# RetNet recurrence and SwiGLU block on one core: first chunk's scores first, and a new table of times for the later stages

## The chip, the cores and the metric

The kernel runs on one core of one Trainium2 chip. The metric is the device time of one execution, in microseconds (us). The engines are named as in the profile: PE is TensorE's matrix multiply and PEld its load of weights, DVE is VectorE, ACT is ScalarE, POOL is GpSimd, SP is SyncE, whose queue issues all the DMA transfers of this kernel. Each engine works through its own list of instructions in order; an instruction that waits holds up all behind it on the same engine.

## The reference

Two blocks follow one another. The first is a RetNet recurrence over 4 batches, 8 heads, 768 positions and 64 features of a head; the second is a SwiGLU feed-forward block on the 3072 x 512 matrix that comes out of it.

```python
gamma = 1.0 - 2.0 ** (-5.0 - np.arange(H))
scale = 1.0 / np.sqrt(D)
for t in range(S):
    state = gamma[None, :, None, None] * state + np.einsum('bhd,bhe->bhde', k[:, :, t], v[:, :, t])
    y[:, :, t] = scale * np.einsum('bhd,bhde->bhe', q[:, :, t], state)
# (B,H,S,D) -> (B*S, H*D), then
g = x @ w_gate                       # 3072 x 1536
silu = g * (1.0 / (1.0 + np.exp(-g)))
out = (silu * (x @ w_val)) @ w_out   # 3072 x 512
```

q, k and v are float32, the three weight matrices float64.

## The kernel before

**Chunks and segments.** The recurrence is done in chunks of 128 positions (6 to a batch): *scores* of a chunk (keys against queries, times a decay mask), a *mix* (scores against values, plus the decayed query against the state before), and a new *state* (decayed keys against values). A segment is 3 chunks of each of 2 batches; there are 4 segments, s = 0 to 3. Each goes through an *up* stage (gate and value products, 12 groups f of 128 hidden columns) and a *down* stage (12 groups f against six tiles of 128 tokens, `tok`). The attention of segment s + 1 is laid between the matmuls of the down stage of segment s. So the time runs: opening (attention of segment 0), up 0, down 0, up 1, down 1, up 2, down 2, up 3, down 3.

**Opening and first up stage.** The order of the opening is the string `START`. Each word is a step of `parts`: `l2:1` loads operand 1 of chunk number 2 (0 is k transposed, 1 q transposed, 2 v, 3 k), `A0` a slice of the table of decays (`tabs`), `s` scores, `m` mix, `t` state, `K`/`k` and `Q`/`q` the scaling of keys and queries by decays (capital: on DVE, small: on POOL), `g` the decay of a state, `x0:1` one sum of x, `U1:2` the load of weight piece 1 into buffer place 2, `a`, `b`, `S`, `c`, `C` the steps that turn float64 words into float32 (`a`, `b`, `c` on ACT, `S` on DVE, `C` on POOL), `T` sums of weights, `w6` six matmuls of filler. The table of decays is `tab`: columns 0 to 1023 are the mask, in two halves of 512 for the two heads of a pair, then the decays of queries and keys. `scores` (L412) does 16 matmuls into two banks and then two DVE multiplies (L424), one for each half of the mask; there are two banks for scores of all chunks. The first up stage (`up`, L653, matmuls L663) multiplies in plain float32; between its products `beside` names what else is done, mostly the conversion of the weights. A load that overwrites a buffer waits in SP's queue until the last reader is through, and all loads behind it wait as well.

**Later stages.** Matmuls run in a faster 32-bit form on operands cut in three parts. Weights and hidden values are cut by `near_a` (ACT, L718), `near_b` (DVE, L721) and `near_c` (POOL, L724, or DVE, L80); x is cut by `far_a` to `far_d` (ACT L727, DVE L80, DVE L733, ACT L739). An up stage (`up3`, L828, matmuls L824) does seven products for each f in the order 1, 2, 6, 5, 7, 3, 4, of 6 matmuls each, after a scheme that saves one product in eight; the results are added up by `p1`, `u2`, `p5` (ACT copies, L839 to L841), `c11`, `h1`, `h0` (DVE additions), and two silus and two multiplies:

```python
        steps = (lambda: copy(p1, x), lambda: tt(c11, z, p1, op=add),
                 lambda: act(gate, c11, AF.Silu, scale=ONE), lambda: copy(u2, x),
                 lambda: copy(p5, wb), lambda: tt(h1, x, p5, op=add),
                 lambda: tt(h0, wb, u2, op=add), lambda: tt(h0, h0, gate, op=mul),
                 lambda: act(x, x, AF.Silu, scale=ONE), lambda: tt(h1, h1, x, op=mul))
        for d, step in zip(WHEN["u", 3 if f == NF - 1 else min(f, 2)], steps):
            at(t + d, step)
```

Products 6, 7 and 4 add to the bank of product 1, so product 6 waits for p1's copy and product 7 for u2's. Split weights and hidden values take turns in four buffers (`item("g", ...)`).

**What sets the order.** `at(t, fn)` files a step under a time; `run()` emits all steps sorted by it. These times are not waits: they only say in which order each engine has its instructions. The table `WHEN` has the times, as offsets from the start of the work they belong to: `('u', i)` the ten steps above (i is f, 2 for f from 2 to 10, 3 for the last), `('w', i, g)` the three steps of cutting weight group g, `('h', f)` those of hidden group f before `down`, `('s', p, g)`, `('m', p)`, `('y', p)`, `('old', p)`, `('new', p)`, `('sum', p)` and `('far', p, n)` what follows scores, mix and state of the p-th pair of chunks in a down stage, `'end'` and `'last'` the evictions of the down stage's results. Before the change nearly all keys of one kind have the same times.

Of the kernel before, what the change touches and what calls it, by code (L numbers as in the profile page):

```python
# [49 lines left out]
def tile_retnet_swiglu(  # L50
# [233 lines left out]
    def do(order):  # L284
# [7 lines left out]
        l0:0 l0:1 A0 l1:0 l1:1 l0:2 l1:2 A1 l0:3 l2:0 l2:1 l1:3 l2:2 l2:3 l3:0 l3:1 l3:2  # L292
        l3:3 l4:0 l4:1 U0:0 l4:2 l5:0 l5:1 l5:2 l4:3 l5:3 s1 s0 K0 m1 w6 k2 K1 t0 m0 s2 t1
        g3 Q2 g2 x0:0 x0:1 s3 U1:2 q3 m2 m3 t2 x1:0 k3 a0 x0:2 x0:3 t3 b0 x1:1 s4 S0 q4 x1:2
        c0 s5 q5 x1:3 m4 C0 m5 a1 x2:0 U3:4 T0:0 x2:1 T0:1 U2:0 T0:2 x2:2 x2:3 U12:6
# [30 lines left out]
        ('u', 0): (1.15, 2.19, 2.89, 3.24, 4.29, 5.33, 6.38, 7.08, 7.43, 8.13),  # L326
        ('u', 1): (1.15, 2.19, 2.89, 3.24, 4.29, 5.33, 6.38, 7.08, 7.43, 8.13),
        ('u', 2): (1.15, 2.19, 2.89, 3.24, 4.29, 5.33, 6.38, 7.08, 7.43, 8.13),
        ('u', 3): (1.15, 2.19, 2.89, 3.24, 4.29, 5.33, 6.38, 7.08, 7.43, 8.13),
        ('w', 0, 0): (-9.0, -7.4, -6.2),  # L330
        ('w', 0, 1): (-9.0, -7.4, -6.2),
        ('w', 0, 2): (-9.0, -7.4, -6.2),
        ('w', 1, 0): (-7.2, -5.6, -4.4),
        ('w', 1, 1): (-7.2, -5.6, -4.4),
        ('w', 1, 2): (-7.2, -5.6, -4.4),
        ('w', 2, 0): (-7.2, -5.6, -4.4),
        ('w', 2, 1): (-7.2, -5.6, -4.4),
        ('w', 2, 2): (-7.2, -5.6, -4.4),
        ('h', 0): (-7.5, -6.3, -5.3),
        ('h', 1): (-7.5, -6.3, -5.3),  # L340
        ('h', 2): (-7.5, -6.3, -5.3),
        ('h', 3): (-7.5, -6.3, -5.3),
        ('h', 4): (-7.5, -6.3, -5.3),
        ('h', 5): (-7.5, -6.3, -5.3),
        ('h', 6): (-7.5, -6.3, -5.3),
        ('h', 7): (-7.5, -6.3, -5.3),
        ('h', 8): (-7.5, -6.3, -5.3),
        ('h', 9): (-7.5, -6.3, -5.3),
        ('h', 10): (-7.5, -6.3, -5.3),
        ('h', 11): (-7.5, -6.3, -5.3),  # L350
        ('s', 0, 0): (0.0, 0.0),
        ('s', 0, 1): (0.0, 0.0, 0.0, 0.0),
        ('m', 0): (0.0, 0.0, 0.0),
        ('y', 0): (0.0, 0.0, 0.0, 0.0, 0.0, 0.0, 0.0, 0.0),
        ('old', 0): 2.4,
        ('new', 0): 0.0,
        ('sum', 0): (2.6, 3.0, 3.4, 3.8),
        ('far', 0, 1): (2.8, 4.6, 5.2, 6.0),
        ('far', 0, 2): (3.5, 5.8, 6.2, 6.8),
        ('far', 0, 0): (4.2, 6.5, 9.2, 10.6),  # L360
        ('s', 1, 0): (0.0, 0.0),
        ('s', 1, 1): (0.0, 0.0, 0.0, 0.0),
        ('m', 1): (0.0, 0.0, 0.0),
        ('y', 1): (0.0, 0.0, 0.0, 0.0, 0.0, 0.0, 0.0, 0.0),
        ('old', 1): 2.4,
        ('new', 1): 0.0,
        ('sum', 1): (2.6, 3.0, 3.4, 3.8),
        ('far', 1, 1): (2.8, 4.6, 5.2, 6.0),
        ('far', 1, 2): (3.5, 5.8, 6.2, 6.8),
        ('far', 1, 0): (4.2, 6.5, 9.2, 10.6),  # L370
        ('s', 2, 0): (0.0, 0.0),
        ('s', 2, 1): (0.0, 0.0, 0.0, 0.0),
        ('m', 2): (0.0, 0.0, 0.0),
        ('y', 2): (0.0, 0.0, 0.0, 0.0, 0.0, 0.0, 0.0, 0.0),
        ('old', 2): 2.4,
        ('new', 2): 0.0,
        ('sum', 2): (2.6, 3.0, 3.4, 3.8),
        ('far', 2, 1): (2.8, 4.3, 4.9, 5.6),
        ('far', 2, 2): (3.5, 5.2, 5.6, 6.0),
        ('far', 2, 0): (4.2, 6.1, 6.9, 8.0),  # L380
        'end': (0.1, 0.1, 0.1, 0.1, 5.0, 5.0),
        'last': (0.1, 0.1, 0.1, 0.1, 0.1, 0.1),
# [671 lines left out]
```

## Time and profile before

| | before |
|---|---|
| time, median of 3 | 695.98 us (695.15 to 696.91) |
| span of the profiled execution | 691.8 us, 12321 instructions |
| PE busy | 666.2 us (96%), 4724 matmuls |
| PEld busy | 551.0 us (80%) |
| DVE busy | 474.9 us (69%), 742 instructions |
| ACT busy | 382.5 us (55%), 793 instructions |
| POOL busy | 250.3 us (36%), 164 instructions |
| DMA | 141.58 MB, 205 GB/s over the span |
| granted PE clock | 1.00 throughout |

The span is the time from the first to the last instruction that the profiler saw. Busy times of different engines overlap. A busy PE isn't PE at its peak, since matmuls are pipelined and their ends are modelled; a wait between two groups of matmuls shows as idle time or as a longer group. The stages can be told by PE's lines: L418 to L478 opening, L663 first up stage, L874 with L520 a down stage with attention, L824 a later up stage.

### The profile page before, as it was taken

The numbers are of one execution on the slowest core, as the hardware profiler recorded it, in microseconds if no ns is written. First come the engines' busy times: TensorE is split into PE (matmuls) and PEld (weight loads), VectorE is DVE, ScalarE is ACT, GpSimd is POOL, SyncE is SP. The second block draws the span as 40 slices with busy tenths as digits, with TensorE's granted clock in tenths as the row PEclk, the third lists the DMA queues.
The fourth block names the chain that finished last, engine by engine and source line by source line (L and its number), as shares of the span: only waits on it lengthen the run. The fifth ranks groups of instructions, "written<-read, shape, count | busy, mean of one in ns | idle before, by whom it ended". The sixth has DMA issues, their size and how long they took to land.

```text
span 691.8 us, 12321 instructions
## 1 busy us (share of the span) xinstructions
PE 666.2 (96%) x4724; PEld 551.0 (80%) x4724; DVE 474.9 (69%) x742; ACT 382.5 (55%) x793; POOL 250.3 (36%) x164
## 2 busy tenths in 40 slices
PE   6899899999999999999999999999999999999997
PEld 5755455567678899997777899998777799999885
DVE  2558998985887766665777767666577867667541
ACT  1488879755556454553578555554464645555111
POOL 0334557640112666640110665661011465562000
PEclk9999999999999999999999999999999999999999
DMA  8689899966574543364756433264756453313553
GB/s 316 230 309 335 313 328 400 397 226 216 202 253 169 196 146 107 132 217 162 249 203 220 170 137 116 98 205 168 232 180 213 194 190 126 140 54 119 196 188 136
DMA packets 49578, 141.58 MB, mean 205 GB/s; under 512 B 6128, under 2 KB 18928, under 8 KB 49520
## 3 DMA queue, kind: packets, MB, share of 16 engines
q1 hardware_dynamic: 49520, 140.80, 58.6%
q8 instruction: 37, 0.61, 0.3%
q14 instruction: 21, 0.17, 0.1%
HBM read 114.04 MB, written 26.74 MB: 204 GB/s over the span
## 4 chain that ended last, share of the span: by engine, by line
PE 64%; DVE 17%; ACT 9%; issue 4%; DMA 3%; SPq 1%; POOL 0%; DVEq 0%; ACTq 0%; POOLq 0%
PE bank L824 34%; PE bank L874 14%; PE bank L663 9%; PE bank L520 4%; ACT chunk_x L759 4%; DVE gitem L721 3%; DVE x L733 2%; DVE x L80 2%; DMA rawp<-in_w_gate_dram 2%; DVE tmp L80 1%; DVE gitem L80 1%; PE bank L418 1%; ACT gitem L718 1%; DVE chunk_x L885 1%; DVE tmp L539 1%
## 5 line engine op out<-in xcount | busy, mean ns | idle before, releaser
L824 PE MATMUL bank<-x,gitem 128*128 128x384 f32 x1296 | 233.7, 336 | 3.8 <-ACT tmp L840 3.8
L824 PEld LDWEIGHTS bank<-x,gitem 128*128 128x128 f32 x1296 | 225.6, 188 | 6.9 <-ACT tmp L840 5.7
L874 PE MATMUL bank<-oitem,gitem 128*128 128x512 f32 x864 | 214.5, 401 | 0.0
L874 PEld LDWEIGHTS bank<-oitem,gitem 128*128 128x128 f32 x864 | 158.8, 188 | 40.3 <-issue 2.9
L724 POOL TENSOR_TENSOR gitem<-gitem 128x768 fp32r<-128x768 f32 x72 | 136.1, 1890 | 132.4 <-DVE gitem L721 132.4
L721 DVE SCALAR_TENSOR_TENSOR gitem<-gitem,loads 128x768 fp32r<-128x768 f32 x72 | 74.1, 1029 | 62.8 <-ACT gitem L718 62.8
L663 PE MATMUL bank<-first 128*128 128x384 f32 x336 | 110.9, 489 | 3.2 <-DVE hT L696 2.2
L663 PEld LDWEIGHTS bank<-first 128*128 128x128 f32 x336 | 62.8, 190 | 49.4 <-DVE hT L696 3.1
L721 DVE SCALAR_TENSOR_TENSOR gitem<-gitem,hT 128x768 fp32r<-128x768 f32 x48 | 46.2, 963 | 46.7 <-ACT gitem L718 46.4
L593 POOL TENSOR_TENSOR loads<-loads,tab 128x512 f32<-128x512 f32 x8 | 15.0, 1879 | 156.5 <-PE bank L520 156.5
L718 ACT ACTIVATE gitem<-loads 128x768 fp32r<-128x768 f32 x72 | 60.8, 844 | 0.0
L843 ACT ACTIVATE bank<-bank 128x384 f32<-128x384 f32 x36 | 17.1, 475 | 78.3 <-PE bank L824 78.3
L718 ACT ACTIVATE gitem<-hT 128x768 fp32r<-128x768 f32 x48 | 39.6, 838 | 25.9 <-PE bank L874 25.8
L232 POOL TENSOR_TENSOR first<-first,rawp 128x1024 int32<-128x1024 int32 (+1 forms) x21 | 41.4, 1975 | 34.4 <-DVE first L223 17.9
L80 DVE SCALAR_TENSOR_TENSOR gitem<-gitem 128x768 fp32r<-128x768 f32 x48 | 45.8, 954 | 1.0
L759 ACT COPY chunk_x<-bank 64x256 f32<-64x256 f32 x72 | 26.5, 368 | 35.6 <-PE bank L520 33.6
L824 PE MATMUL bank<-x,oitem 128*128 128x384 f32 x216 | 44.0, 339 | 1.3 <-DVE hT L841 1.3
L840 ACT ACTIVATE bank<-tmp 128x384 f32<-128x384 f32 x36 | 17.8, 496 | 48.1 <-DVE tmp L839 48.1
L739 ACT ACTIVATE x<-x 128x512 fp32r<-128x512 f32 (+2 forms) x27 | 18.9, 700 | 37.8 <-DVE x L733 37.8
L824 PEld LDWEIGHTS bank<-x,oitem 128*128 128x128 f32 x216 | 36.8, 188 | 3.2 <-DVE hT L841 2.3
L724 POOL TENSOR_TENSOR oitem<-oitem 128x256 fp32r<-128x256 f32 x36 | 28.6, 794 | 15.2 <-DVE oitem L721 13.5
L520 PEld LDWEIGHTS bank<-loads 64*64 64x64 f32 (+1 forms) x800 | 22.6, 134 | 13.8 <-issue 5.1
(93 smaller groups left out, 738.3 us busy)
## 6 DMA issues: line engine op xcount, KB each, us to landing
oitem<-wdnt SPq DMA_DIRECT2D x45, 768.0 KB, 4.3
loads<-wup SPq DMA_DIRECT2D x36, 896.0 KB, 4.7
wup<-first SPq DMA_DIRECT2D x12, 896.0 KB, 7.4
wdnt<-oitem SPq DMA_DIRECT2D x12, 768.0 KB, 5.5
rawp<-in_w_val_dram SPq DMA_DIRECT2D x24, 256.0 KB, 5.5
rawp<-in_w_gate_dram SPq DMA_DIRECT2D x12, 512.0 KB, 6.5
out_dram<-chunk_x SPq DMA_DIRECT2D x24, 256.0 KB, 2.1
loads<-in_k_t_dram SPq DMA_DIRECT2D x18, 256.0 KB, 4.4
```

The costliest lines, as they stand in the source:

```text
L80: stt(o, x, 1.0, y, op0=mul, op1=op)
L232: pool(d[:, ts(i, n)].bitcast(I32), d[:, ts(i, n)].bitcast(I32), lo[:, ts(i, n)].bitcast(I32), op=add)
L520: nc.tensor.matmul(o, a, b, start=start, stop=True, skip_group_check=True)
L663: nc.tensor.matmul(o, w[:, slot, k], a[:, k], start=(start and k == 0), stop=(stop and k == KH - 1), skip_group_check=True)
L718: act(o[0], x, AF.Copy, scale=CUT / FAR)
L721: stt(o[1], f32(o[0]), -FAR, x, op0=mul, op1=add)
L724: op(o[2], f32(o[0]), f32(o[1]), op=add)
L739: act(o[2], f32(o[2]), AF.Copy, scale=FAR / ONE)
L759: copy(cx[half[i], ds(2 * h, 2), c], y_both(h, i, c))
L824: nc.tensor.matmul(o, w[:, a, k], xs_of[s][:, a, OP[p], k], start=start and a == k == 0, stop=a == 2 and k == KH - 1, skip_group_check=True)
L840: lambda: act(gate, c11, AF.Silu, scale=ONE), lambda: copy(u2, x),
L874: nc.tensor.matmul(banks[tok], hs[f][:, a, ds(i * TH + u * P, P)], wo[f][:, a], start=f == a == 0, stop=f == NF - 1 and a == 2, skip_group ...
```

## The change

Two parts. In the opening, chunk 0's scores are computed first, where chunk 1's were; the mask is loaded as two transfers of 256 KB, one for each half of the scores' multiply, where it was one of 512 KB; and the order of the steps behind is written anew: the load of weights 1 comes ahead of the last two loads of keys, the load of weights 2 ahead of that of weights 3 and before the last mix. `beside`, which orders the first up stage, stays as it was.

In the later stages the offsets of `WHEN` are set one by one for each kind, pair and group. No instruction is added or taken away there; their order on each engine changes. The hidden groups of the last down stage get a row of their own, ('h', 12), with the old times.

```diff
     START = """
-        l0:0 l0:1 A0 l1:0 l1:1 l0:2 l1:2 A1 l0:3 l2:0 l2:1 l1:3 l2:2 l2:3 l3:0 l3:1 l3:2
-        l3:3 l4:0 l4:1 U0:0 l4:2 l5:0 l5:1 l5:2 l4:3 l5:3 s1 s0 K0 m1 w6 k2 K1 t0 m0 s2 t1
-        g3 Q2 g2 x0:0 x0:1 s3 U1:2 q3 m2 m3 t2 x1:0 k3 a0 x0:2 x0:3 t3 b0 x1:1 s4 S0 q4 x1:2
-        c0 s5 q5 x1:3 m4 C0 m5 a1 x2:0 U3:4 T0:0 x2:1 T0:1 U2:0 T0:2 x2:2 x2:3 U12:6
+        l0:0 l0:1 A0 A1 l1:0 l1:1 l0:2 l1:2 A2 l0:3 l2:0 l2:1 l1:3 l2:2 l2:3 l3:0 l3:1 l3:2
+        l3:3 l4:0 l4:1 U0:0 l4:2 l5:0 l5:1 l5:2 U1:2 l4:3 l5:3 s0 w6 s1 m0 m1 K0 t0 K1 s2 t1
+        g2 g3 Q2 s3 m2 x0:0 x0:1 x0:2 x0:3 k2 q3 t2 s4 a0 b0 m3 k3 t3 q4 c0 s5 S0 x1:0 x1:1
+        x1:2 x1:3 m4 a1 q5 C0 U2:0 m5 x2:0 T0:0 x2:1 T0:1 x2:2 x2:3 T0:2 U3:4 U12:6
     """
...
     WHEN = {
-        ('u', 0): (1.15, 2.19, 2.89, 3.24, 4.29, 5.33, 6.38, 7.08, 7.43, 8.13),
...
-        ('u', 3): (1.15, 2.19, 2.89, 3.24, 4.29, 5.33, 6.38, 7.08, 7.43, 8.13),
-        ('w', 0, 0): (-9.0, -7.4, -6.2),
-        ('w', 0, 1): (-9.0, -7.4, -6.2),
...
-        ('w', 2, 0): (-7.2, -5.6, -4.4),
...
-        ('h', 11): (-7.5, -6.3, -5.3),
-        ('s', 0, 0): (0.0, 0.0),
...
-        ('far', 2, 0): (4.2, 6.1, 6.9, 8.0),
-        'end': (0.1, 0.1, 0.1, 0.1, 5.0, 5.0),
+        ('u', 0): (1.15, 2.16, 2.86, 3.39, 4.9, 5.3, 8.05, 13.63, 7.4, 8.1),
+        ('u', 1): (0.41, 2.51, 3.16, 3.92, 4.38, 5.59, 6.95, 8.3, 7.26, 12.66),
+        ('u', 2): (0.33, 1.32, 3.61, 3.15, 4.0, 5.51, 5.85, 6.13, 7.28, 7.66),
+        ('u', 3): (1.63, 1.81, 3.34, 2.86, 3.53, 5.07, 6.18, 7.14, 7.05, 7.54),
+        ('w', 0, 0): (-11.39, -6.27, -4.75),
+        ('w', 0, 1): (-7.89, -7.84, -1.53),
+        ('w', 0, 2): (-10.42, -10.31, -9.95),
+        ('w', 1, 0): (-9.1, -4.79, -3.1),
+        ('w', 1, 1): (-7.91, -6.99, -4.78),
...
+        ('w', 2, 0): (-7.82, -4.49, -3.72),
+        ('w', 2, 1): (-11.06, -7.92, -6.85),
+        ('w', 2, 2): (-9.26, -5.23, -3.28),
+        ('h', 0): (-7.38, -5.56, -4.85),
+        ('h', 1): (-9.84, -9.24, -1.21),
+        ('h', 2): (-7.15, -3.81, -2.2),
...
+        ('h', 4): (-13.19, -12.55, -12.11),
...
+        ('h', 6): (-7.31, -2.68, -1.02),
+        ('h', 7): (-9.96, -8.79, -6.96),
...
+        ('s', 1, 1): (0.78, 1.54, 2.46, 2.56),
+        ('m', 1): (-1.08, -6.39, -1.02),
...
+        ('old', 1): -5.96,
+        ('new', 1): 0.83,
...
+        ('far', 2, 1): (2.61, 4.22, 4.91, 8.85),
+        ('far', 2, 2): (3.64, 4.9, 5.88, 10.4),
+        ('far', 2, 0): (4.41, 5.29, 9.73, 11.99),
+        'end': (1.36, -0.0, 0.1, 1.03, 7.96, 4.59),
         'last': (0.1, 0.1, 0.1, 0.1, 0.1, 0.1),
+        ('h', 12): (-7.5, -6.3, -5.3),
     }
...
-            h_split(steps[f], f)
+            h_split(steps[f], f, f if nxt else NF)
...
-    tabs = slice(0, QDEC0), slice(QDEC0, NTAB)
+    tabs = slice(0, QDEC0 // 2), slice(QDEC0 // 2, QDEC0), slice(QDEC0, NTAB)
```

Offsets of `('u', ...)` count from the first product of f; those of `('w', i, g)` from the product that first uses the group (0, 3.14 and 6.28 us after it for g = 0, 1, 2 in the plan's own times, in which one f lasts 7.33); those of `('h', f)` from the first matmul of group f in the down stage.

## The prediction

> **What bounds the kernel now.** I read the busy time of each engine by stage first, then TensorE's waits, then the order of work around each wait. Stage windows (columns: window, length, busy time of each engine, clock, DMA):
>
> ```profile
> core 0: us, PE busy (x) PEld busy (x) DVE busy (x) ACT busy (x) POOL busy (x), PEclk, DMA share, GB/s
> 0.00:36.50 36.50, 28.71 (x348) 24.84 (x348) 14.80 (x28) 10.44 (x21) 8.58 (x11) 1.00 0.75 260
> 36.50:150.00 113.50, 110.28 (x369) 63.29 (x365) 96.56 (x158) 90.34 (x161) 62.18 (x37) 1.00 0.93 340
> 150.00:222.40 72.40, 70.58 (x766) 53.90 (x765) 53.00 (x82) 41.14 (x97) 8.01 (x4) 1.00 0.64 214
> 222.40:313.00 90.60, 88.76 (x505) 87.18 (x504) 61.75 (x99) 48.07 (x98) 52.29 (x36) 1.00 0.45 156
> ...
> 637.00:691.80 54.80, 50.55 (x217) 40.35 (x215) 22.35 (x26) 10.52 (x14) 0.00 (x0) 1.00 0.51 173
> ```
>
> TensorE (PE) bounds every stage after the first: 36.5 us of opening, 113.5 of first up stage, then down and up by turns. So the change can win only what PE waits. The table of waits, PE alone:
>
> ```profile
> PE bank L418 <- DMA hT<-in_q_t_dram: 4.2, 1, 4.2
> PE bank L824 <- ACT tmp L840: 3.8, 6, 1.1
> PE bank L520 <- DVE loads L80: 3.1, 3, 1.0
> PE bank L663 <- DVE hT L696: 2.2, 1, 2.2
> PE bank L418 <- DVE tmp L424: 1.7, 3, 0.8
> PE bank L824 <- DVE hT L841: 1.3, 3, 0.4
> PE bank L520 <- DVE states L628: 1.1, 2, 0.5
> ```
>
> One wait each is in the opening (4.2) and in the first up stage (2.2); the others fall at the same places of every later stage. PE's order of time, in two places (the bracket is the idle time ahead):
>
> ```profile
> 222.42 4.50 PE L824 MATMUL bank<-x,gitem 128*128 128x384 f32 x24
> 227.95 2.42 PE L824 MATMUL bank<-x,gitem 128*128 128x384 f32 x12 [1.04 <-ACT tmp L840]
> 230.81 1.31 PE L824 MATMUL bank<-x,oitem 128*128 128x384 f32 x6 [0.44 <-DVE hT L841]
> ...
> 314.58 1.53 PE L520 MATMUL bank<-loads 64*64 64x128 f32 x32
> ...
> 408.06 6.43 PE L824 MATMUL bank<-x,gitem 128*128 128x384 f32 x36
> 414.33 1.21 PE L824 MATMUL bank<-x,oitem 128*128 128x384 f32 x6
> 415.38 6.43 PE L824 MATMUL bank<-x,gitem 128*128 128x384 f32 x36
> ```
>
> Inside an up stage one f takes 415.38 - 408.06 = 7.32 us without a gap: 12 x 7.32 = 87.8. The three up stages take 90.7, 90.1 and 90.8, so each loses 2.3 to 3.0, all at its two ends. Scores (L520, 32 matmuls) take 0.90 undisturbed; the 1.53 above hides a wait of 0.63. Recoverable altogether: about 8.5 us of up stages, 1.3 of such scores, some 2 in each of three down stages, 3.2 in the first up stage, and the opening.
>
> **What the Trainium skill says.** "Perfetto Trace Analysis", Optimization Strategy: find the gaps of the bounding engine, see which instruction's semaphore ends them, and make that dependency start sooner; that is the reading above. "SBUF — State Buffer", Who interferes with whom: a VectorE instruction with two SBUF inputs and a GpSimd one that reads SBUF exclude each other. The trace agrees: a split step (L721) that takes 0.95 took 2.61 beside GpSimd's 2.77 (usually 1.84). "DMA: Bandwidth & Descriptors", Queues, rings and completion order: the loads of one issuing engine are consumed in ring order. In the trace the first two loads land 2.7 and 2.8 us after issue, those behind the 512 KB mask 6.1 and 6.3.
>
> **The opening.** Before, chunk 1's scores come first; its operands, behind chunk 0's and the whole mask, land at 2.59 + 6.30 = 8.89, and PE starts at 9.03. Chunk 0's q lands at 1.19 + 2.8 = 4.0. The change starts with its scores, so PE goes on at 4.9, when the eight warm-up matmuls (to 4.83) are through: 4.9 to 7.0. Its evictions need mask halves: the second lands with the old single load at 7.55, the first between, about 5.8. VectorE is through at 7.8 and 8.4. The added DMA issue costs the queue 0.45 us. Then, by lines of before (scores 1.16 warm, mix 1.02 or 2.05 with a state, state 0.69):
> - scores 1 at 8.9 to 11.0 (operands); mixes 0 and 1 to 13.6; state 0 to 14.3 (key scaling K0 on VectorE done 13.4); scores 2 to 15.5, state 1 to 16.2.
> - scores 3 at 16.9 (VectorE has emptied the two score banks) to 18.1, mix 2 to 20.1, state 2 to 20.8, scores 4 to 22.0, mix 3 to 24.1, state 3 to 24.8.
> - scores 5 need their q, which lands about 24.5; 24.8 to 26.0; mixes 4 and 5 to 30.1.
>
> Before, the last mix ended at 36.6. GpSimd's conversion of the first weights (C0, 2 x 1.27) needs the VectorE step S0, about 28.6, so its first half is there at 29.9 and its second at 31.1. First up product at 30.2 instead of 36.57, and about 0.4 lost before the second product (sums of the second half on VectorE): **-5.9**. Both ends: -6.4 if nothing else bites, -4 if U1, now ahead of two chunk loads, and the conversions put ACT and GpSimd a step behind.
>
> **First up stage.** Its one long wait (2.24 at 86.15) ends a chain: load of weights 2 (issued 38.20, landed 44.62), conversion, buffer free, next load (53.89 to 61.07), then VectorE without a pause from 72 to 88. The change issues load 2 ahead of load 3, as soon as C0 is done, about 31 to 32, some 6.5 us earlier, against PE's 5.9. So the wait shrinks by about one: **-1.0** (0 to -2; +2 if conversions on VectorE, busy 96.6 of 113.5, don't move with PE).
>
> **Start of each later up stage.** PE waits for u2's copy (L840), which sits on ACT behind silu(c11), which waits for c11 on VectorE, which sits behind split steps:
>
> ```profile
> 220.81 2.61 DVE L721 SCALAR_TENSOR_TENSOR gitem<-gitem,loads 128x768 fp32r<-128x768 f32 x1
> 223.34 1.27 DVE L885 TENSOR_SCALAR chunk_x<-bank 128x512 f32<-128x512 f32 x2
> 224.54 1.08 DVE L721 SCALAR_TENSOR_TENSOR oitem<-oitem,loads 128x256 fp32r<-128x256 f32 x1
> 225.55 0.95 DVE L721 SCALAR_TENSOR_TENSOR gitem<-gitem,loads 128x768 fp32r<-128x768 f32 x1
> 226.42 0.55 DVE L839 TENSOR_TENSOR tmp<-bank,tmp 128x384 f32<-128x384 f32 x1
> ```
>
> The new table moves the split of f=1 behind c11 (times 2.54 and 2.16; before 1.73 and 2.19), 0.95 off VectorE's queue, and f=1's ACT step ahead of the silu, into an idle stretch of 2.5. Against it, x's last part ('far' 2,0) now finishes late: its third step on VectorE behind three weight splits, about 223.3 to 224.0 with the GpSimd conflict, then 1.06 on ACT, and p1's copy, which the third product at 224.7 needs, sits behind it: a new wait of 0.3 to 1.0. Old waits 1.04 + 0.44 and some 0.2 of restart (12 matmuls in 2.42 there, 2.1 undisturbed), new 0.7: -1.0, three times: **-3.0** (-4.5 to 0).
>
> **End of each later up stage.** In the last f's row the copy of u2 comes ahead of silu (-4.47, -3.99; before silu first), and of h1's split only one step stands ahead of c11: the 0.36 to 0.37 wait goes, -0.4 x 3 = **-1.2**. The 0.63 in the first scores is bank 7, still read by f=11's last multiply, queued behind the split of h1; that split's second step now comes after (3.89 instead of -0.20): -0.6 in two stages: **-1.2**.
>
> **Inside the down stages.** The split of h4 moves into VectorE's idle 6 us ahead of x's sums, so the state and the scaled q of the second pair (waits 0.54 and 1.02, and 0.45 hidden in scores) come up to 1.9 earlier; q's scaling still meets GpSimd's other half (2.0): 0.4 stays. New risk: h7's split is put between fence and h6's, on ACT behind eight key scalings (1.96); after its own 0.84 there come four VectorE steps of 0.95, h7's and h6's by turns, so h6 is ready about 189.7 where PE wants it at 188.4: 1.3 new. First pair's q scaling moves behind h2's first step: up to 0.5 new in two stages. Net about -0.2 each, **-0.5** (-4 to +4).
>
> **Middle of the up stages.** f=2 to 10 keep PE saturated: in the new order per 7.32 us VectorE has 5.1 us of work, ACT 4.5, GpSimd 4.45; weights are split over 3 us ahead of use, and u2's copy follows its product at once. Nothing: hidden beside matmuls. The last down stage keeps its times (row 12 has the old ones): nothing.
>
> Sum: -5.9 - 1.0 - 3.0 - 1.2 - 1.2 - 0.5 = -12.8; 695.98 - 12.8 = 683.2.
>
> **Rivals.** (A) A new wait takes the old one's place: 'far' 2,0 and h6 stall at their full size, and conversions don't keep up in the first up stage. Then up-stage starts give 0 rather than -3.0, down stages +2 rather than -0.5, the first up stage +1: 695.98 - 5.9 + 1 - 1.2 - 1.2 + 2 = 690.7; with an opening of -4, 692.6. For it: VectorE's full queue at each boundary. Against: the moves go into idle stretches that the timelines show. (B) The new order removes nearly all: opening -6.4, first up -2, up starts -4.5, ends -2.4, down -2: 678.7. (C) Slower: a wait that recurs with each middle f, 27 of them; 0.5 each is +13.5, against the opening's -5.9, the other gains lost: 703.6. A buffer of the ring of four freed too late would do it: the split of f starts 0.4 us after the last use of its slot. Against it: that order is met without a wait. (D) The opening is hidden anyway because weights, not PE, set the first up stage: -12.8 + 5.9 = 690.1.
>
> **How the numbers follow.** Forecast (about 680.5 to 686.5) 0.50, A 0.15, D 0.11, B 0.16, C 0.06, no change 0.02. Range 678 to 691: it takes in B's and most of A's and D's, leaving out B's tail, C and A's worse end. Faster: all but C and no change, 0.92.
>
> **What would show it.** First scores of the chunks at about 4.9 and the first up product (L663) at 30 to 31; L840 no longer ahead of PE's waits, at most a shorter one at the third product of each up stage; up stages of 88.5 to 89.8; the first scores after an up stage at 0.9; a wait of about 1 for h6 (L80 gitem) in the down stages. Wrong if the first up stage grows beyond 115, or if f=3 to 10 take more than 7.35.

## The result, and the profile after

The changed kernel takes 674.42 us (median of 4, 672.58 to 676.0) where the kernel before took 695.77 beside it: a ratio of 0.969, interval 0.9662 to 0.9719, faster. That lies below the forecast's range. The span of the profiled execution went from 691.8 to 672.9. Line numbers from the chunk code on are one higher than before (L824 is now L825).

The stage windows of the changed kernel, columns as before (window, length, busy time of PE, PEld, DVE, ACT, POOL, clock, DMA share and rate):

```profile
core 0: us, PE busy (x) PEld busy (x) DVE busy (x) ACT busy (x) POOL busy (x), PEclk, DMA share, GB/s
0.00:29.50 29.50, 25.58 (x349) 22.63 (x349) 15.32 (x28) 11.37 (x22) 7.52 (x11) 1.00 0.91 313
29.50:146.50 117.00, 112.01 (x366) 63.79 (x365) 96.61 (x159) 89.23 (x160) 63.40 (x38) 0.99 0.91 332
146.50:216.00 69.50, 69.50 (x767) 53.56 (x766) 52.21 (x85) 41.86 (x100) 7.97 (x4) 1.00 0.67 223
216.00:303.80 87.80, 87.80 (x505) 87.67 (x504) 59.45 (x97) 49.02 (x95) 52.71 (x36) 1.00 0.47 161
303.80:374.10 70.30, 68.46 (x763) 52.85 (x762) 50.56 (x80) 45.50 (x116) 7.68 (x5) 1.00 0.61 205
```

The first down stage and the first of the later up stages have no idle PE left (69.50 of 69.50, 87.80 of 87.80). The first up stage is longer than before, 117.0 for 113.5, and its clock is below 1. All stages, in us, from the start of one stage's first matmul to the next's:

| | opening | up 0 | down | up 1 | down | up 2 | down | up 3 | last down |
|---|---|---|---|---|---|---|---|---|---|
| before | 36.57 | 113.31 | 72.54 | 90.66 | 71.40 | 90.10 | 71.59 | 90.82 | 54.81 |
| after | 29.48 | 117.02 | 69.48 | 87.86 | 70.24 | 87.92 | 67.90 | 88.22 | 54.78 |
| difference | -7.09 | +3.71 | -3.06 | -2.80 | -1.16 | -2.18 | -3.69 | -2.60 | -0.03 |

So 18.9 us went: 7.6 in the later up stages, 7.9 in the down stages, 3.4 in the opening and first up stage together. The waits of PE after (us in total, times, longest):

```profile
PE bank L664 <- DVE hT L697: 3.7, 2, 2.3
PE bank L521 <- ACT chunk_x L760: 1.8, 1, 1.8
PE bank L419 <- DMA hT<-in_q_t_dram: 1.3, 1, 1.3
PE bank L419 <- DMA rawp<-in_q_t_dram: 1.2, 1, 1.2
```

The waits for u2's copy (L840 before) and for the scaled queries (DVE loads L80) are gone, and neither p1's copy nor h6 appears in their place. New are a second wait in the first up stage and one of 1.84 in the second down stage. PE's order of time, in the opening (start, busy time, the bracket is idle time ahead):

```profile
4.76 2.07 PE L419 MATMUL bank<-hT 64*128 64x128 f32 x16
...
15.78 1.16 PE L419 MATMUL bank<-hT 64*128 64x128 f32 x16 [1.29 <-DMA hT<-in_q_t_dram]
...
24.30 1.16 PE L419 MATMUL bank<-rawp 64*128 64x128 f32 x16 [1.24 <-DMA rawp<-in_q_t_dram]
...
29.48 1.56 PE L664 MATMUL bank<-first 128*128 128x384 f32 x4
```

The first scores run at 4.76 and the first up product at 29.48; the forecast had 4.9 and 30.2. What PE still waits for there is queries.

Part of the opening's gain is clock. Before the change, what followed the wait of 4.20 ran at half speed, as the same step of scores shows early and late:

```profile
9.03 2.08 PE L418 MATMUL bank<-hT 64*128 64x128 f32 x16 [4.20 <-DMA hT<-in_q_t_dram]
...
19.36 1.16 PE L418 MATMUL bank<-hT 64*128 64x128 f32 x16
```

The record of the clock in that execution starts only at 16.26, so its mean of 1.00 says nothing of these steps. The kernel with the old opening and the new table (below) has nearly the same durations there, and its record shows a clock of 0.5 from 8.87 to 15.70. In the changed kernel only the first scores are slow (2.07, and 1.16 for the next at 8.30). An estimate from these durations: two scores and a mix lost 0.9 each before, one step of scores 0.9 after, so about 1.8 of the 7.1 is clock.

### The profile page after: what moved, and what is told of

It is laid out like the page before. It is cut to its first block, busy times and chain, and to the rows that moved or that the text cites. A ratio compares the mean times of both kernels' runs of the same rounds, so it can differ in the third digit from the quotient of the medians.

```text
span 672.9 us, 12402 instructions
## 1 busy us (share of the span) xinstructions
PE 658.1 (98%) x4724; PEld 548.8 (82%) x4724; DVE 466.1 (69%) x742; ACT 386.7 (57%) x793; POOL 250.5 (37%) x164
## 4 chain that ended last, share of the span: by engine, by line
PE 85%; DMA 7%; DVE 3%; ACT 3%; issue 1%; POOL 1%; SPq 0%; DVEq 0%; ACTq 0%; POOLq 0%
PE bank L825 39%; PE bank L875 28%; PE bank L664 10%; PE bank L521 6%; DMA loads<-wup 1%; DMA rawp<-in_q_t_dram 1%; DMA rawp<-in_w_gate_dram 1%; DVE first L80 1%; DMA rawp<-in_w_val_dram 1%; DMA hT<-in_k_n_dram 1%; DMA hT<-in_k_t_dram 1%; ACT rawp L217 1%; DMA tab<-in_decays_dram 1%; POOL gitem L725 1%; DVE oitem L738 0%
## 5 line engine op out<-in xcount | busy, mean ns | idle before, releaser
L825 PE MATMUL bank<-x,gitem 128*128 128x384 f32 x1296 | 231.8, 335 | 0.1
L825 PEld LDWEIGHTS bank<-x,gitem 128*128 128x128 f32 x1296 | 225.8, 188 | 1.2 <-POOL gitem L725 0.4
L875 PE MATMUL bank<-oitem,gitem 128*128 128x512 f32 x864 | 214.8, 401 | 0.2 <-DVE hT L843 0.2
L725 POOL TENSOR_TENSOR gitem<-gitem 128x768 fp32r<-128x768 f32 x72 | 138.6, 1946 | 119.0 <-DVE gitem L722 112.5
L664 PE MATMUL bank<-first 128*128 128x384 f32 x336 | 112.9, 495 | 5.0 <-DVE hT L697 3.7
L719 ACT ACTIVATE gitem<-loads 128x768 fp32r<-128x768 f32 x72 | 57.9, 840 | 36.4 <-issue 30.8
L594 POOL TENSOR_TENSOR loads<-loads,tab 128x512 f32<-128x512 f32 x8 | 12.7, 1591 | 142.7 <-PE bank L521 142.7
L722 DVE SCALAR_TENSOR_TENSOR gitem<-gitem,loads 128x768 fp32r<-128x768 f32 x72 | 65.5, 951 | 0.0
L80 DVE SCALAR_TENSOR_TENSOR gitem<-gitem 128x768 fp32r<-128x768 f32 x48 | 46.0, 963 | 0.8
L760 ACT COPY chunk_x<-bank 64x256 f32<-64x256 f32 x72 | 25.6, 368 | 34.8 <-PE bank L521 34.1
L841 ACT COPY tmp<-bank 128x384 f32<-128x384 f32 x36 | 17.2, 479 | 46.3 <-PE bank L825 44.6
L825 PE MATMUL bank<-x,oitem 128*128 128x384 f32 x216 | 43.8, 338 | 0.0
L842 DVE TENSOR_TENSOR hT<-bank,tmp 128x384 f32<-128x384 f32 x36 | 20.1, 558 | 27.1 <-PE bank L825 27.1
L844 DVE TENSOR_TENSOR hT<-hT,bank 128x384 f32<-128x384 f32 x36 | 19.9, 553 | 26.8 <-ACT bank L844 26.8
L825 PEld LDWEIGHTS bank<-x,oitem 128*128 128x128 f32 x216 | 38.0, 188 | 0.0
L840 DVE TENSOR_TENSOR tmp<-bank,tmp 128x384 f32<-128x384 f32 x36 | 20.1, 557 | 19.2 <-PE bank L825 19.2
```

Source lines behind the costliest of these rows:

```text
L80: stt(o, x, 1.0, y, op0=mul, op1=op)
L664: nc.tensor.matmul(o, w[:, slot, k], a[:, k], start=(start and k == 0), stop=(stop and k == KH - 1), skip_group_check=True)
L719: act(o[0], x, AF.Copy, scale=CUT / FAR)
L722: stt(o[1], f32(o[0]), -FAR, x, op0=mul, op1=add)
L725: op(o[2], f32(o[0]), f32(o[1]), op=add)
L760: copy(cx[half[i], ds(2 * h, 2), c], y_both(h, i, c))
```

## The experiments

The stage lengths below are read as in the table above, each from the one profiled execution of a kernel. The two halves of the change, the filler, weights 4 and the two kernels with fixes were also timed several times; the other kernels have that one execution alone, so they are compared stage by stage. The time of one kernel differs by some us from execution to execution; the stages without a wait repeat within about 0.1.

**The two halves of the change alone.** One kernel has the new opening with the old table of times, the other the old opening with the new table.

```text
opening only:  START and tabs of the changed kernel, all else as before
table only:    all of the changed kernel but START and tabs, which are as before
```

> The new opening alone, the old table of times. Theory (supply): the weights' loads and conversions, not the matmuls, set the first 50 us of the first up stage, and they come only 5.0 us earlier (the end of the long wait moved from 86.15 to 81.11); so 695.8 - 5.0 = 690.8, or 692.5 if TensorE's clock drops again for 3.4 us after that wait. Rival (the opening's 7.1 us are kept whole and the longer first up stage comes from elsewhere, the table or the clock): 688.7.

> The new table alone, the old opening. Theory (the order of the later stages is good for all their waits, whatever the opening): 695.8 - 15.7 = 680.1, with up stages of 87.9 and down stages of 69.5, 70.2 and 67.9. Rival (the prediction: part of the later gain is given back in new waits, -5.9): 689.9. Rival (part of the later gain comes from the opening's shift of the loads): between, 683 or more.

The opening alone gave 690.18 (687.45 to 693.37), ratio 0.9928, interval 0.9908 to 0.9947, between the theory's 690.8 and the rival's 688.7 and too scattered to decide. The opening took 29.53 (-7.0), the first up stage 115.81 (+2.5), this without a halved clock. All later stages kept their waits, and their lengths within 0.15. The table alone gave 680.55 (679.75 to 682.95), ratio 0.9793, interval 0.9767 to 0.9819: down and up stages of 69.48, 87.83, 72.50, 87.87, 67.90, 88.15, opening and first up stage 36.03 and 113.35 (before: 36.57 and 113.31). That is the theory's 680.1, with one stage apart: the second down stage of 72.50 (below). About 70% of the gain is the table's, and the first up stage takes back a third of what the opening gives.

**Filler at the end of the opening.** Eight groups of filler, 2.0 us of PE, ahead of the first up product.

```diff
-x1:2 x1:3 m4 a1 q5 C0 U2:0 m5 x2:0
+x1:2 x1:3 m4 a1 q5 C0 U2:0 m5 w8 x2:0
```

> The changed kernel with eight more pairs of filler matmuls (16 x 0.133 = 2.1 us) between the last mix and the first up product. Theory (supply): the first up stage's waits, 5.0 us in all, take them in; the wait before 81.11 ends at the same time: 674.4 to 675.0. Rival (matmuls set the first up stage): 676.5.

The opening took 31.48 (+2.0) and the first up stage 113.58; together 145.06. The changed kernel has 146.50, of which 1.7 is a clock at half rate that didn't come here (last section); so counted it has 144.8, and seven other kernels with these two stages unchanged (opening only, old h, u, w, u and w, attention, x between) 144.3 to 145.3. So PE's extra 2.0 us cost 0.3, at most 0.8: starting the first up stage earlier is worth little. The wait at 59.8 for h1 (L697) shrank from 1.42 to 0.41, so a part of the filler only fills that wait; that the weights, which don't come sooner, are what holds the stage back is likely and not shown. The time, 677.6 (675.74 to 678.91), missed both expectations. In the profiled execution, the fastest of its four (675.74), the second down stage accounts for that: the wait for chunk_x was 2.9 there and the clock halved after it.

**Weights 4 asked for earlier.**

```diff
-g5 g4 C1 | ...  T3:1 F12:0 U4:2 Z2
+g5 g4 C1 U4:2 | ...  T3:1 F12:0 Z2
```

> The changed kernel with the load of weights 4 issued behind the conversion of weights 1 that frees its buffer, ahead of the load of weights 5, instead of behind it. Theory (supply): ScalarE no longer waits for weights 4 at 56.2, the wait of 1.42 before 59.83 goes, and the long one before 81.11 shrinks: 671.5 to 673. Rival (VectorE's own work sets the long wait): the 1.42 goes but reappears before 81: 674.4.

The wait of 1.42 went and the first up stage took 115.57, 1.5 less. The time stayed as it was, 674.47 (673.25 to 678.78), ratio 0.9711 (0.9674 to 0.9748); in the profiled execution the second down stage had a wait of 5.27. The long wait, now ahead of 79.08, stayed at 2.24, as neither expectation had it. It is 2.22 to 2.27 in every kernel of these experiments except the last two with fixes, whatever was done to loads and opening, so it doesn't hang on the supply of weights. VectorE's order of time in the changed kernel shows on what:

```profile
77.69 0.54 DVE L694 TENSOR_TENSOR hT<-bank,tmp 128x384 f32<-128x384 f32 x1
78.16 2.43 DVE L80 SCALAR_TENSOR_TENSOR first<-first 128x256 f32<-128x256 f32 x3
80.51 0.55 DVE L697 TENSOR_TENSOR hT<-bank,tmp 128x384 f32<-128x384 f32 x1
```

Three sums of weights (L80, `T5:2 T6:0 T6:1`) stand between h0 (L694) and h1 (L697) in the order of VectorE, and PE's next product in that bank waits for h1. They take 2.43 beside a GpSimd step of 1.61, where such a sum alone takes 0.41. The same order stood there before the change:

```profile
83.20 2.43 DVE L80 SCALAR_TENSOR_TENSOR first<-first 128x256 f32<-128x256 f32 x3
85.55 0.54 DVE L696 TENSOR_TENSOR hT<-bank,tmp 128x384 f32<-128x384 f32 x1
```

**One kind of rows at a time as before.** In four kernels the new table keeps all but one or two kinds of its rows; in two more, groups of kinds are old.

```text
old h:         ('h', f) as before
old u:         ('u', i) as before
old w:         ('w', i, g), ('far', 2, n), 'end' as before
old u and w:   the last two together as before
old att:       ('s'), ('m'), ('y'), ('old'), ('new'), ('sum'), ('far', 0 and 1) as before
old h and att: both as before
```

> The changed kernel with the old times of the hidden groups ('h'). Theory (h4's cut ahead of x's sums is what lets VectorE be early in the down stages): the waits on the state (0.54) and on the scaled query (1.02) come back, and with them the one hidden in scores; each down stage 2 to 3 us longer, the up stages the same. Rival (the gain of the down stages is spread over the attention's own times): under 1 us each.

> The changed kernel with the old times of the up stages' ten steps ('u'). Theory (these rows matter only at the last f, where u2's copy now comes ahead of silu): the wait of 0.37 before the last products comes back, 0.3 to 0.6 us in each of three up stages, their starts stay clean. Rival (the rows also set the starts): 1.5 us and more each.

> The changed kernel with the old times of the weights' cuts, of the last pair's x and of the evictions ('w', 'far' 2, 'end'). Theory (these set the start of the up stages): the waits for u2's copy and h1 come back, 1.5 to 2.3 us in each up stage, down stages the same; one cut on VectorE takes about 2.6 us again beside GpSimd. Rival (VectorE's lead from the down stage is enough): under 0.5 us each.

> The changed kernel with the rows for the up stages' steps (u) and for the stages' ends and beginnings (w, the third pair's far, end) as before; the rows for h and attention stay new. Theory that these rows carry the later up stages' gain only as a pair: up stages 90.5 to 91 again, with the waits of 1.04 and 0.43 at their starts back and every middle f at 7.32, so 3 x 2.8 = 8.4 us lost, a span of 681 (the span of the changed kernel is 672.9). Rival, that the gain comes from VectorE being earlier into these stages through the h and attention rows: the up stages stay at 88 to 88.5 and the span at or below 674. The old w rows with new u rows lost 11 us per stage, old u with new w rows nothing: neither alone says what the old pair gives.

> The changed kernel with the attention rows (s, m, y, old, new, sum, far of the first two pairs) as before. Theory that the h rows and the attention rows add: with the h rows old the first and third down stage were 1.34 and 1.84 longer than in the changed kernel, and 1.72 and 1.85 remain to the kernel before, so here 71.2 and 69.75; and the wait of 1.8 to 5.3 in the second down stage, which comes from the third pair's keys being asked for late, goes, so that stage is 69.5 to 71 and the clock isn't halved there. Rival, that the two sets of rows only work together: first and third stage within 0.4 of 72.54 and 71.59. Up stages 88 either way.

> The changed kernel with the h rows and the attention rows both as before; u, w, the third pair's far and end stay new. With both old rows for u and w the up stages took 89.74, 88.37 and 90.28 where 87.9 is new and 90.1 to 90.8 is old. Theory that the rest, 0.6 to 2 a stage, comes from VectorE's lead out of the down stages: up stages 88.5 to 89.3 here. Rival, that the lead does nothing once the u and w rows fit each other: 87.9 to 88.2. Down stages by both: 72.5, 71.4 and 71.6 as before, since the two sets gave 0.8 to 1.8 each of 3.1 and 3.7 and 0.9 came with either alone.

Stage lengths measured (us), with the spans; "all old" and "all new" are the kernels before and after:

| | down | up 1 | down | up 2 | down | up 3 | span |
|---|---|---|---|---|---|---|---|
| all new | 69.48 | 87.86 | 70.24 | 87.92 | 67.90 | 88.22 | 672.9 |
| old h | 70.82 | 87.91 | 75.30 | 87.88 | 69.74 | 87.92 | 680.9 |
| old att | 70.29 | 88.52 | 68.82 | 88.65 | 68.85 | 88.55 | 674.5 |
| old h and att | 72.53 | 88.23 | 71.26 | 88.42 | 71.46 | 88.24 | 683.3 |
| old u | 69.49 | 87.76 | 70.74 | 87.92 | 67.90 | 88.80 | 671.3 |
| old w | 69.48 | 99.26 | 74.71 | 98.49 | 67.90 | 99.33 | 708.5 |
| old u and w | 69.47 | 89.74 | 73.96 | 88.37 | 67.91 | 90.28 | 681.4 |
| all old | 72.54 | 90.66 | 71.40 | 90.10 | 71.59 | 90.82 | 691.8 |

*Down stages.* With h and attention rows both old, all three stages are as before within 0.15, so these two kinds of rows are the whole of the gain. They don't add: old h alone costs 1.3 and 1.8 in the first and third, old attention alone 0.8 and 1.0, both 3.1 and 3.6. What comes only when both are old is the wait for scaled queries:

```profile
PE bank L521 <- DVE loads L80: 3.1, 3, 1.0
...
PE bank L521 <- DVE states L629: 1.1, 2, 0.5
```

These are the waits of the kernel with both old, the same as before the change; with either kind new the first line is missing. The expectation that the two would add missed by 0.9 a stage. With the attention rows alone old, a wait for h6 (L80 gitem) appears, 0.36 in the first stage and 0.48 in the third.

The second down stage is apart: wherever the attention rows are new and the third pair's are not mended, a wait of 1.8 to 5.3 for chunk_x stands in it, in some kernels with a halved clock behind it; with old attention rows that wait is gone (68.82). The changed kernel's 70.24 is the shortest of those that have all its down-stage rows: six others (table only, filler, weights 4 early, old u, and x between and the mask as one load below) took 70.7 to 76.1. So in this stage the new rows can as well lose as win against the 71.40 before. More on it below.

*Up stages.* With h and attention rows old but u and w new, the up stages take 88.2 to 88.4: 2.4, 1.7 and 2.6 of the 2.8, 2.2 and 2.6 are there. So the up stages' own rows are enough for nearly all. What VectorE is earlier out of the down stages (its *lead*) adds at most 0.5 to them. The mirror image, old u and w with the lead, takes 89.74, 88.37 and 90.28, with the old waits back, but 0.67 and 0.42 where there were 1.04 and 0.44. Its start of up 1, PE:

```profile
221.41 2.43 PE L825 MATMUL bank<-x,gitem 128*128 128x384 f32 x12 [0.67 <-ACT tmp L841]
224.26 1.31 PE L825 MATMUL bank<-x,oitem 128*128 128x384 f32 x6 [0.42 <-DVE hT L842]
```

So the lead alone gives 0.9, 1.7 and 0.5 of what the old rows lose, and the new rows need little of it: the two overlap. The u rows alone matter in one place (0.6 at the end of up 3, a wait of 0.47 for L841). Old w rows under new u rows are a case by themselves, missed by far: each middle f takes 8.29 in place of 7.32, since h1 comes late 27 times:

```profile
255.09 1.31 PE L825 MATMUL bank<-x,oitem 128*128 128x384 f32 x6 [0.37 <-DVE hT L842]
256.24 6.77 PE L825 MATMUL bank<-x,gitem 128*128 128x384 f32 x36
263.38 1.31 PE L825 MATMUL bank<-x,oitem 128*128 128x384 f32 x6 [0.38 <-DVE hT L842]
```

A visible wait of 0.37 stands for 0.97 of time: PE's 36 matmuls also take 6.77 in place of 6.43, and the six after the wait 1.31 in place of 1.21. VectorE has h1 (L842) right behind a cut of weights, which takes 1.97 in place of 0.95; a GpSimd step of 1.83 had begun 0.67 ahead of it:

```profile
252.59 1.97 DVE L722 SCALAR_TENSOR_TENSOR gitem<-gitem,loads 128x768 fp32r<-128x768 f32 x1 [0.85 <-ACT gitem L719]
254.49 0.55 DVE L842 TENSOR_TENSOR hT<-bank,tmp 128x384 f32<-128x384 f32 x1
```

This is the recurring wait that rival C feared, 27 times over, though not through a buffer freed too late, as C supposed, but through the order on VectorE. The old u and w rows together have no such wait, nor have the new ones; only the mixture has.

**Where x's last step stands.** The forecast had put it at 223.3 to 224.0 on VectorE, 0.9 to 1.6 behind the start of the up stage. In the changed kernel (start of the up stage 215.98), VectorE:

```profile
211.61 1.82 DVE L722 SCALAR_TENSOR_TENSOR gitem<-gitem,loads 128x768 fp32r<-128x768 f32 x2
213.34 0.41 DVE L722 SCALAR_TENSOR_TENSOR oitem<-oitem,loads 128x256 fp32r<-128x256 f32 x1
213.68 1.22 DVE L734 SCALAR_TENSOR_TENSOR x<-x 128x1024 fp32r<-128x1024 f32 x1
```

Two weight cuts take 0.91 each, the third 0.41, and x's step is through at 214.9, 1.1 before the stage starts. The price is paid by GpSimd, whose step takes 3.91 where 1.84 is usual:

```profile
212.70 3.91 POOL L725 TENSOR_TENSOR gitem<-gitem 128x768 fp32r<-128x768 f32 x1 [16.93 <-DVE gitem L722]
```

With the old w rows x's step stands between two cuts, and there VectorE pays:

```profile
210.76 1.22 DVE L734 SCALAR_TENSOR_TENSOR x<-x 128x1024 fp32r<-128x1024 f32 x1
211.90 2.61 DVE L722 SCALAR_TENSOR_TENSOR gitem<-gitem,loads 128x768 fp32r<-128x768 f32 x1
```

The Trainium skill ("SBUF — State Buffer", Who interferes with whom) calls this an exclusive lock, which whoever issues first has for the whole instruction. The sums agree: GpSimd's 3.91 ends 1.8 after VectorE's row of two-input steps ends (214.8), its own full time; VectorE's 2.61 is GpSimd's rest, 211.9 to 213.6, and 0.95. Why GpSimd got in between in the one order and not in the other these records don't settle. An attempt to put x's step between the cuts in the changed kernel missed its mark, since the step came out ahead of both; so it doesn't test its theory. The cuts stayed at 0.91, GpSimd's step took 2.78 and again ended 1.8 after VectorE's row (214.33), and the up stages stayed as they were (span 672.8):

```diff
-('far', 2, 0): (4.41, 5.29, 9.73, 11.99),
+('far', 2, 0): (4.41, 5.29, 7.4, 11.99),
```

> The changed kernel with one step of x (the third of 'far' 2,0) put between the first and second cut of weights on VectorE, where it was before the change. Theory (whichever of VectorE and GpSimd comes first holds up the other): the second cut now finds GpSimd at work, takes about 2.6 us instead of 0.95, and GpSimd's first sum goes from 3.9 to about 2.8; the up stages start with a wait of at most 0.5 or none. Rival (VectorE's cuts are short because GpSimd starts later): the cut stays near 0.95.

**The mask as one load.**

```diff
-l0:0 l0:1 A0 A1 l1:0 l1:1 l0:2 l1:2 A2 ...   tabs of QDEC0 // 2
+l0:0 l0:1 A0 l1:0 l1:1 l0:2 l1:2 A1 ...      tabs of QDEC0
```

> The changed kernel with the mask of the first chunk loaded as one transfer of 512 KB in place of two of 256 KB. Theory that the order of the first scores carries the opening's gain and the halves little: the opening is 29.5 to 29.8 and PE's first waits 0 to 0.3 longer. Rival, that the halves let the first scores start: the opening is 31.2 or more, 1.7 us longer, with a wait of PE or VectorE for the mask's load.

The opening took 31.87, 2.4 longer, with a wait of 1.44 for the first multiply by the mask, which no kernel with the halves has, and a span of 676.1. But 1.7 of the 2.4 is the clock at half rate from 19 to 22.4, after a wait of 2.63 for queries; the rest is 0.7, since PE waits less for queries afterwards (the wait of 1.24 at 24.3 is gone). Nor is the length of one opening proof: with old h and attention rows, whose opening is that of the changed kernel, the wait for queries was 2.67 and the opening 32.0. Opening and first up stage together, less 1.7 for the halved clock, are 146.6 here, where eight kernels with the halves have 144.3 to 145.3. So the halves matter, by 1.3 to 2.3 us in this one execution; that is more than the theory had, and in the opening itself less than the rival's 1.7.

**Fixes for the waits left.** Two kernels put weights 4 and two of the three sums elsewhere, and change the third pair's rows in the down stages. In the first of them the third pair's state stands four places later, behind the load that takes its values' place, so it is computed from weights: the same instructions on other data, a reading of waits and no kernel to keep. In the second it is one place later, ahead of that load.

```diff
-g5 g4 C1 | ... F12:0 U4:2 Z2 | ... T5:2 T6:0 T6:1 Z12 | S7
+g5 g4 C1 U4:2 | ... F12:0 Z2 | ... T5:2 Z12 | T6:0 T6:1 S7
-('m', 2): (-0.66, 3.25, -0.35),   ('new', 2): 5.62,
+('m', 2): (-0.66, 3.25, 1.4),     ('new', 2): 2.9 (four fixes), 4.9 (three)
-PARTS[b + n] = what, p, g
+PARTS[b + n + 4 * (what == "t" and p == 2)] = ...      (three: 1 * )
```

The two kernels' edits are shown as one here, shortened; they differ where two values stand.

> The changed kernel with four edits, each at one of the waits left: the load U4:2 eleven places earlier (the 1.42 wait at 59.8 goes, 1.4 us), two sums moved from behind h0 to behind h1 of the first up stage (most of the 2.27 wait goes, 1.5 to 2.2 us, and with it the half clock for 3.4 us after it, 1.7 us), and in the second down stage the third pair's state four places later, its mask and new copies at other times (the 1.84 wait and a half clock after it in some runs, 1.8 to 3). Theory that these waits are separate: 669 to 671, ratio 0.961 to 0.965. Rival, that a wait moved aside comes back at the next place (as the third pair's load did in the second down stage): 673 to 676, 0.968 to 0.972, as the changed kernel.

> As the run with four fixes, but the third pair's state stands one place later, ahead of the load of up weights that takes the place of its values, and its new-state row is 4.9. In the run with four fixes the state stood behind that load and so read weights in place of the values. Theory that its wait of 1.78 in the second down stage was for that load: here the copies of the third pair's output end at about 360.5 by the changed kernel's record less 1.9, so the state waits 0 to 0.4, the second down stage is 68.4 to 69.0, the first up stage 114.9 as there, and the time 669 to 671.5. Rival, that a wait of about 2 comes back wherever the state stands, since the keys' load lands when it lands: 70 or more in this stage, and 672 to 675.

The first took 672.12 (670.52 to 673.24), ratio 0.9662 (0.9641 to 0.9683), between its two expectations, with a wait of 1.78 ahead of the state in the second down stage. The second took 671.02 (670.24 to 672.07), ratio 0.9663 (0.9639 to 0.9688), and a span of 668.7: first up stage 114.79 (-2.2), second down stage 69.05 (-1.2), with a wait of 0.71 left ahead of the state. VectorE's order around h1, in this kernel:

```profile
75.90 0.55 DVE L694 TENSOR_TENSOR hT<-bank,tmp 128x384 f32<-128x384 f32 x1
76.36 0.41 DVE L80 SCALAR_TENSOR_TENSOR first<-first 128x256 f32<-128x256 f32 x1
76.70 0.55 DVE L697 TENSOR_TENSOR hT<-bank,tmp 128x384 f32<-128x384 f32 x1
```

One sum in place of three, and the wait for h1 is 0.22 in place of 2.27. So the three sums were its cause. Yet of 1.42 and 2.27 of waits and 1.7 of halved clock only 2.2 came off the stage, because others grew:

```profile
PE bank L664 <- ACT tmp L688: 1.8, 3, 0.8
PE bank L664 <- ACT tmp L691: 1.4, 1, 1.4
```

Less the halved clock, the kernel with weights 4 alone moved needs 113.9 for this stage, and this one 114.8: moving the sums won no time beyond the halved clock that it avoids.

In the second down stage the new rows of the changed kernel put the scaling of one half of the third pair's keys ahead of other work on ScalarE (the bracket is its idle time):

```profile
353.77 2.02 ACT L602 ACTIVATE loads<-loads,tab 128x64 f32<-128x64 f32 x8 [7.50 <-DMA loads<-in_k_n_dram]
355.70 0.83 ACT L719 ACTIVATE gitem<-hT 128x768 fp32r<-128x768 f32 x1
356.44 1.04 ACT L740 ACTIVATE x<-x 128x1024 fp32r<-128x1024 f32 x1
357.39 2.00 ACT L602 ACTIVATE loads<-loads,tab 128x64 f32<-128x64 f32 x8
359.41 2.92 ACT L760 COPY chunk_x<-bank 64x256 f32<-64x256 f32 x8
```

ScalarE stands still for 7.5 us until the keys' load lands, with a cut and a step of x queued behind the first scaling; these and the second scaling then push the end of the copies of the bank (L760) to 362.3, and PE's state waits for them. With the three fixes the cut and the step of x aren't between the scalings any more:

```profile
352.53 3.93 ACT L602 ACTIVATE loads<-loads,tab 128x64 f32<-128x64 f32 x16 [4.42 <-DMA loads<-in_k_n_dram]
356.49 2.92 ACT L760 COPY chunk_x<-bank 64x256 f32<-64x256 f32 x8
```

The copies now begin 4.0 after the first scaling in place of 5.6, and 15 matmuls stand ahead of the state in place of 12. So the order is worth 1.7 on ScalarE and 0.7 on PE, an estimate from these lines; the two weren't tried apart. But the wait also follows the landing of the keys, as the rival had it: they land 49.8 us after the start of this stage in the changed kernel, 50.5 with the table only, 51.6 with old w, 53.2 with weights 4 early, and the waits there are 1.84, 2.57, 3.67 and 5.27. With the three fixes they land at 51.0, and 0.71 of wait is left; with old attention rows they land at 51.4, and no wait stands there at all. So the landing sets how long the wait is, and the order whether there is one. In all these kernels the load is asked for 46.1 to 46.9 after the stage's start; why it lands so unevenly is open. The expected 68.4 to 69.0 for the stage was missed by 0.05, the expected wait of at most 0.4 by 0.3. That the kernel with three fixes is faster than the changed one is likely, but its size is open: they weren't run side by side, and the intervals of their ratios overlap.

## Why the prediction was wrong

The direction, the mechanism of the opening and the end of the old waits in the later stages were right; the size was not: -12.8 forecast, -18.9 in the spans. The terms of the sum miss by more than their total. The opening won 1.2 more than forecast, the later up stages 3.4 more and the down stages 6.2 more, while the first up stage lost 4.7 that were not forecast; that this loss hid nearly half of the rest is luck. Of the 8.8 by which the time was missed, 6.1 is this. A further 2.4 comes from the base: the waits were read from an execution of before that took 693.57, that much under its median of 695.98. The last 0.3 is the changed kernel's profiled execution, that much above its median.

- **Opening**, forecast -5.9, measured -7.1. The order held, and so did both ends (scores 0 at 4.76 for 4.9, first product 29.48 for 30.2). In between PE ran 0.5 to 1.9 ahead of the forecast, and waited for queries where the forecast had none (1.29 at 15.78, 1.24 at 24.30). That about 1.8 of the gain is clock it didn't say.
- **First up stage**, forecast -1.0, measured +3.7. The step that failed is "its one long wait ends a chain" of weight loads: the wait kept its 2.2 in every kernel until two sums were moved on VectorE, so it never hung on that chain; it hung on three sums (2.43) ahead of h1 on VectorE, which the forecast had seen only as "VectorE without a pause". The rest is rival D in part: weights 4 gave a new wait of 1.42, filler in the opening cost at most 0.8, and the halved clock added 1.7. The stage's 117.0 is beyond the 115 that the prediction had named as a sign of being wrong.
- **Start and end of each later up stage**, forecast -1.0 and -0.4, measured -2.8, -2.2 and -2.6 together. Two terms were mis-sized. The new wait of 0.3 to 1.0, counted as 0.7, for p1's copy isn't there, because the cuts ahead of x's step take 0.91 and 0.41, and GpSimd, not VectorE, gives way. And the losses beside the named waits were put at 0.2, although nearly all that stood above 12 x 7.32 = 87.8 could go, and went. This is what rival B had said of these stages.
- **Down stages**, first scores -1.2 and inside -0.5 forecast, -7.9 measured. This is the largest miss. The step that failed is the new waits, which left "net about -0.2 each": the forecast kept 0.4 for scaled queries and set 1.3 for h6 and 0.5 for the first pair's queries, and in the changed kernel none came. It had even named "some 2" in each stage as recoverable and then forecast next to none of it; the first and third stage gave 3.1 and 3.7. The first scores did come down to 0.90 as forecast, and the waits that the forecast had found (0.54, 1.02 and 0.45) went whole; the remaining 1.1 in each of these two stages no run assigns. That the 1.3 for h6 was wrong shows in VectorE's order in the first down stage of the changed kernel:

```profile
179.78 0.42 DVE L584 COPY warm<-bank 128x1 f32<-128x1 f32 x2 [2.79 <-PE bank L521]
180.95 1.83 DVE L722 SCALAR_TENSOR_TENSOR gitem<-gitem,hT 128x768 fp32r<-128x768 f32 x2 [0.75 <-ACT gitem L719]
182.70 1.82 DVE L80 SCALAR_TENSOR_TENSOR gitem<-gitem 128x768 fp32r<-128x768 f32 x2
```

The four steps were counted rightly, but they start at 180.95, and h6 is there at 184.5. The forecast, shifted by the 3.4 us that this stage starts earlier, had 186.3: VectorE is 1.8 further ahead than the forecast took from the old times. With old attention rows it is there at 184.93 in a stage that starts 0.5 earlier, and PE does wait 0.36 for h6; so about half of the 1.8 comes from the attention rows.

- **Middle of the up stages**, nothing, held: 7.32 for each f. The second down stage's new wait of 1.84 was not foreseen.
- **Sums and readings**: rival D's 695.98 - 12.8 + 5.9 is 689.1, not 690.1. The up stages' "about 8.5" is 8.2 by its own three numbers. The opening had more than "one wait": the table shows three for VectorE's multiplies (L424), 1.7 in all.

The common fault, as far as the runs show it, is that moves were costed singly against the old times of the other engines. In the down stages, where VectorE is idle for a quarter of the time, the new rows together bring it forward, and the new waits set up from old times were not there. In the first up stage, where it has 96.6 us of work in 113, the opposite held: a wait moved aside came back elsewhere.

## What to carry to other kernels

When steps of a whole stage are laid out anew, price the stage by what its bounding engine loses in sum (length less saturated length), and count a new wait only if it stands on the order of its engine in the new plan, not on the old clock times. Rows that belong together are to be tested in groups: u with w, h with attention; singly, w showed +36 us and u nothing. A wait whose length doesn't change while loads and starts around it move by several microseconds is a local order of instructions, and one move there removes it; whether the stage gets shorter is read from its length, since here other waits grew. A wait whose length follows a load's landing, as that of the second down stage, is not to be judged from one execution.

## What the runs showed of the hardware that had not been expected

PE's clock was halved after some waits, for about 3.4 or 6.8 us, which costs up to half of that. The second down stage took 70.74 after a wait of 2.40 with the clock at full rate (old u), and 72.83 after a wait of 2.90 with 3.4 us at half rate (filler): 0.5 is the longer wait, 1.6 the clock. In the profiled executions of all these kernels the record of the clock covers 27 waits of PE of 2.17 us or more ahead of the last stage; after 16 of them the clock went to 0.5, at the latest 1.4 us behind the restart. After shorter waits, the longest of them 2.09, it never did. One such restart, in the kernel with weights 4 early, begins here, and the clock was 0.5 from 363.0 to 369.8:

```profile
364.12 1.97 PE L521 MATMUL bank<-loads 128*64 128x64 f32 x32 [5.27 <-ACT chunk_x L760]
366.02 6.17 PE L875 MATMUL bank<-oitem,gitem 128*128 128x512 f32 x18
```

The Trainium skill ("TensorE: Matmul & The Clock Gate", What's actually happening) gives half rate after an idle window of about 3.4 us, and full rate again after a busy one of that length. The lengths of the drops agree; the idle time that suffices was shorter here, 2.2 to 2.9 us in 13 of the 16, and not each time (2.24 before: no drop; 2.27 after: a drop). So a wait of 2.2 us was worth up to 3.9, and the two kernels with fixes, with no wait over 1.8, ran at full clock throughout their profiled executions.
